# First batch of an mLSTM and Fourier-mixing kernel: recurrent outputs with tokens on partitions, no transposes, three blocks run backwards

## The chip, the core and the metric

The kernel runs on one core of a Trainium2 chip. The metric is the device time of one execution in microseconds (us). One execution on the chip was also recorded by the profiler: its page and its trace are what the text below reads. TensorE is called PE, its weight loads PEld, VectorE DVE, ScalarE ACT, GpSimd POOL, and SyncE, whose queue starts all the DMAs here, SP.

## What is computed

Two blocks follow each other, each over 4 batches of 768 tokens. The first is an mLSTM cell with 8 heads of 40 features. For each token, with a running maximum `m` that keeps the exponentials in range:

```python
m_new  = maximum(f + m, i)
f_stab, i_stab = exp(f + m - m_new), exp(i - m_new)
C = f_stab * C + i_stab * outer(v, k)      # 40 x 40 per head
n = f_stab * n + i_stab * k
y = sigmoid(o_gate) * (C @ q) / maximum(abs(n @ q), 1)
```

The second takes the heads side by side as `x` (768 x 320 for each batch):

```python
u  = x + real(fft(fft(x, axis=seq), axis=features))
un = (u - mean(u)) / sqrt(var(u) + 1e-6)
out = u + maximum(un @ w_ch1, 0) @ w_ch2   # 320 -> 1280 -> 320
```

The weights `w_ch1` and `w_ch2` arrive as 64-bit floats and are turned into 32-bit ones on the chip.

## The kernel before

**The work of one batch.** The recurrence is done in 6 chunks of 128 tokens. For a chunk, `mlstm_scores` multiplies keys by queries (PE), `mlstm_exp` makes the decay weights from gate sums that `spread_max` has put into PSUM by PE (ACT, 8 activations, one for each head), `mlstm_weigh` multiplies the two (DVE), `mlstm_from_state` adds what the state `C` of earlier chunks gives (PE), `mlstm_from_chunk` what the chunk's own tokens give (PE), and `mlstm_to_state` makes the chunk's part of the next state (PE). `mlstm_decay` (POOL) scales the old state. `mlstm_finish` (DVE, five instructions) divides by the normaliser, applies the output gate that `mlstm_tanh` (ACT) has prepared, and writes 128 tokens x 320 features of `x`.

**The first batch is done in another form than the others.** In batches 1 to 3 (`halves_*`) the outputs come out of PE with the tokens on partitions, 41 columns for each head. In batch 0 (`mlstm_*`, planned by `plan_mlstm`, lines 764 to 782) they come out with features on partitions (line 583, weights `C`, 128 query columns moving; line 590, weights `v1`). ACT then copies them to `hT` (`mlstm_heads`, lines 618 to 632) and copies the state (line 614), and PE turns the copy by four transposes (`mlstm_turn`, line 642) before `mlstm_finish` can read it. The old state is added on PE, by a product with the identity (line 605).

**Mixing.** The Fourier transform over the tokens uses the symmetry of cosines and sines: `mix_fold` adds and subtracts chunk pairs (0,5), (1,4), (2,3), whose second members must lie backwards. In `hT` this was done by ACT's copies, and two tokens (0 and 384) were moved there. `mix_seq` and `mix_tail` (tiles `pz`, `pzt`) transform over tokens, `mix_feat` (tile `pu`) over features, `mix_add` (DVE, lines 966 to 980) adds and takes mean and variance, `mix_center` (ACT, line 988) centres, `mix_turn` (PE, tile `put` or `ph`, line 999) turns, and `mix_turn_out` (ACT, line 1004) copies to `uT`. The two layers of the MLP follow (`mlp_in`, lines 1073 and 1082, then `mlp_out`); the chunks 0, 5, 1 make the first half of its columns, 4, 2, 3 the second.

**Order.** The order on each engine is written by hand. `at(slot, phase, fn, ...)` puts a step into a slot, and `run()` issues the steps in order of slot and phase; each engine takes its instructions in that order, and so does SP with the DMAs. PSUM banks for most of batch 0 are handed out by a string of digits, `turn`. The first batch fills slots 0 to 22, its mixing 22 to 31, its MLP starts in slot 31, and the next batch's recurrence starts in slot 32, between the MLP's products. `gates_of_halves` (lines 319 to 392), in steps 0 to 8, prepares gates for batches 1 to 3. It ran in slots 15 to 22. Its step 2 stores to `M_d` and `G_d` in DRAM what the later batches load, as 12 DMAs and one. The weights come in ten pieces, each with a load (SP), `take` (DVE, two instructions), `convert` (ACT, two) and `join` (DVE, three). The tables of the transform, `ds_sb` (1158 KB) and `dd_sb` (642 KB), are loaded by SP in slot 12, and the output gate of chunk 5 in slot 14.

Of the kernel before, what the change touches and what calls it, by code (L numbers as in the profile page):

```python
# [19 lines left out]
L = 128  # L20
# [17 lines left out]
COL = (0, L + 1, 2 * L + 2)  # L38
LAST = 2 * L + 1
# [4 lines left out]
BACKWARDS = (2, 4, 5)  # L44
# [13 lines left out]
def kernel(  # L58
# [30 lines left out]
    ps_s, ps_h = (ps_early.enter_context(tc.tile_pool(name=n, bufs=2, space=PSUM)) for n in ("ps_s", "ps_h"))  # L89

    turn = iter("3210321032120312031230123102112310231023102310231")
# [7 lines left out]
    rest = const.tile([L, 2 * L], FP, name="rest")  # L99
# [16 lines left out]
    C_bufs = [const.tile([L, NP, L], FP, name=f"C{n}") for n in range(3)]  # L116
    states = [t.rearrange("p n t -> p (n t)")[:, i * 2 * L:(i + 1) * 2 * L] for t in C_bufs for i in range(2)]
# [3 lines left out]
    Cd_bufs = [s_last[:, n * NP * D1:(n + 1) * NP * D1].rearrange("p (n m) -> p n m", m=D1) for n in range(2)]  # L121
    hT_bufs = []
# [18 lines left out]
    def idle_products(n, first=False):  # L141
        pw = bank("pi", [L, 2 * L]) if first else ps_s.tile([L, 2 * L], FP, name="pi", tag="ps")
        for i in range(n):
            nc.tensor.matmul(pw, rest[:, 0:L], rest, start=True, stop=True, skip_group_check=True)


    def gates(gp):
# [3 lines left out]
        hT_bufs.extend(gp.tile([L, NP, L + 1], FP, name=f"h{n}") for n in range(2))  # L151
# [6 lines left out]
        M = gp.tile([L, NT, L], FP, name="M")  # L158
# [6 lines left out]
        ident_b, later_b = (gp.tile([L, L], BF, name=n) for n in ("ident_b", "later_b"))  # L165
# [4 lines left out]
        idle_products(3, True)  # L170
        mlstm_load(0, 0)
        make_identity(nc, ident)
        nc.gpsimd.memset(later_b, 0.0)
# [8 lines left out]
        nc.vector.memset(M[:, 0:2], 0.0)  # L182
        for t in C_bufs:
            nc.scalar.copy(out=t.rearrange("p (two n) t -> p two (n t)", two=2),
                           in_=rest.unsqueeze(1).to_broadcast([L, 2, 2 * L]))
# [8 lines left out]
        for t in hT_bufs + Cd_bufs + alone:  # L194
            nc.gpsimd.memset(t, 0.0)
# [21 lines left out]
        def spread_max(b, c, h0):  # L217

            k = chunks[b, c]
            if h0 == 0:  # L220
                k.W = wp.tile([L, H, L], FP, name="W", tag="W")
                k.M = []
            k.M.append(bank("pM", [L, NP, L]))
            nc.tensor.matmul(k.M[-1], ident_b, later_b.unsqueeze(1).to_broadcast([L, NP, L]), start=True, stop=False,
                             skip_group_check=True)
            for h in range(h0, h0 + NP):
                bh = b * H + h
                w, x = (ident[:, bh:bh + 1], M[:, c, :]) if c < 2 else (sel[:, bh:bh + 1], M3[:, c, :])
                nc.tensor.matmul(k.M[-1][:, h - h0, :], w.to_broadcast([w.shape[0], L]), x, start=False, stop=True,  # L229
                                 skip_group_check=True)  # L230

        def parts(s):

            m, rest_ = M[0:BH, s], shift[:, s]
# [5 lines left out]

        def spread_decay(b, c):
            k = chunks[b, c]
            k.G = bank("pG", [L, NP, L])
            for h in range(H):
                r, bh = slice(h % 2 * 64, (h % 2 + 1) * 64), b * H + h
                nc.tensor.matmul(k.G[r, h // 2, :], ident[:, bh:bh + 1].to_broadcast([L, 64]), g[:, c, :],
# [6 lines left out]
        def decay(s):  # L253
            for c in range(s.start, s.stop):
                nc.scalar.activation(out=g[0:BH, c], in_=M[0:BH, c], func=AF.Exp, scale=-1.0, bias=m_in[:, c])

        def columns(s, j):
            pt = ps_h.tile([L, NT, BH], FP, name="pt", tag="ph")
# [6 lines left out]
        maxima(first, M_INIT)  # L265
        pt = columns(first, 0)
# [34 lines left out]
        def decays():  # L301
            dec = gp.tile([BH, BH // 2, NT], FP, name="dec")
            nc.vector.tensor_tensor(out=dec[:, :, 1:],
                                    in0=g[0:BH, 1:, L - 1].unsqueeze(1).to_broadcast([BH, BH // 2, NT - 1]),
                                    in1=spread_sb[:, L:].unsqueeze(2).to_broadcast([BH, BH // 2, NT - 1]), op=OP.mult)
            pd = bank("pd", [L, BH // 2, NT - 1])
            nc.tensor.matmul(pd, spread_sb[:, 0:L], dec[:, :, 1:], start=True, stop=True)
            late["pd"] = pd

        def decays_out():  # L310
            nc.vector.tensor_copy(out=decB[:, 0:NP, 1:NT], in_=late["pd"][:, 0:NP])
# [4 lines left out]
        def gates_of_halves(step):  # L316
# [15 lines left out]
            elif step == 1:  # L332
                m, w = flat_of(M), W.rearrange("p c (i t) -> p c i t", i=2)
                nc.scalar.copy(out=W[:, 0:4:3].rearrange("p c t -> p c t"),
                               in_=bass.AP(tensor=m.tensor, offset=m.offset + 1, ap=[list(m.ap[0]), [HALF, 2], [1, L]]))
                nc.scalar.copy(out=W[:, 1], in_=M[0:BH, 1])
                for c, n in ((2, 2), (4, 1)):
                    src = bass.AP(tensor=m.tensor, offset=m.offset + START[c] + LH - 1,
                                  ap=[list(m.ap[0])] + ([[HALF, 2]] if n > 1 else []) + [[LH, 2], [-1, LH]])
                    nc.scalar.copy(out=w[:, 2:6:3] if n > 1 else w[:, 4], in_=src)  # L340
                nc.gpsimd.tensor_copy(out=W[:, 0:4:3, L - 1:L], in_=late["nexts"][:, 1:5:3])
                nc.gpsimd.tensor_copy(out=W[:, 4, LH:LH + 1], in_=late["nexts"][:, 5])
            elif step == 2:
                nc.scalar.activation(out=late["between"], in_=late["between"], func=AF.Exp)
                for c in range(NT):
                    for i in range(2):
                        t = slice(i * LH, (i + 1) * LH)
                        nc.scalar.activation(out=G[:, c, t], in_=W[:, c, t], func=AF.Exp, scale=-1.0,
                                             bias=late["starts"][:, c, i:i + 1])
# [8 lines left out]
                nc.sync.dma_start(out=G_d[:, H:].rearrange("c p t -> p c t"), in_=G[H:BH])  # L358
# [35 lines left out]
        at(1, FILL + 0.2, parts, last)  # L394
# [9 lines left out]
        for n, (s, phase) in enumerate(((15, FILL + 0.75), (16, FILL + 0.75), (18, FILL + 0.75), (19, FILL + 0.75),  # L404
                                        (18, FILL + 0.8), (19, FILL_PE + 0.5), (20, FILL + 0.75),
                                        (21, FILL_PE + 0.5), (22, FILL + 0.75))):
# [73 lines left out]
    def mlstm_load(b, c):  # L480
# [3 lines left out]
        k.C = [C_bufs[(i + n) % 3] if b == 0 else states[(b * NS + 2 * c + n) % len(states)] for n in range(3)]  # L484
# [6 lines left out]
        k.kn = k.k[:, 0:H * D].rearrange("p (h d) -> p h d", d=D)  # L491
# [9 lines left out]
    def mlstm_load_decay(b, c):  # L501
        k, t = chunks[b, c], slice(0, L)
        if (b, c) != (0, 0):
            k.Gb = gbp.tile([L, NP, L], FP, name="Gb", tag="Gb")
            for hip in range(2):
                h = slice(hip, H, 2) if b == 0 else slice(b * H + hip * NP, b * H + (hip + 1) * NP)
# [45 lines left out]
    def mlstm_decay(b, c):  # L552

        k = chunks[b, c]
        if 0 < c < NT - 1:
            k.Cd = Cd_bufs[c % 2]
            for hip in range(2):
                r, m = slice(hip * 64, hip * 64 + D), slice(hip * 64, hip * 64 + D1)
                d = decB[r, b * NP:(b + 1) * NP, c].unsqueeze(2).to_broadcast([D, NP, D1])
                nc.gpsimd.tensor_tensor(out=k.Cd[r], in0=k.C[0][r, :, m], in1=d, op=OP.mult)  # L560
# [10 lines left out]
    def mlstm_weigh(b, c):  # L571
        k = chunks[b, c]
        for hip in range(2):
            Wv = k.W.rearrange("p (pr two) t -> p pr two t", two=2)[:, :, hip, :]
            nc.vector.tensor_tensor(out=Wv, in0=k.ps[hip], in1=Wv, op=OP.mult)

    def mlstm_from_state(b, c):

        k = chunks[b, c]
        k.ph = ps_h.tile([L, NP, L], FP, name="ph", tag="ph")  # L580
        if c > 0:
            for p in range(NP):
                nc.tensor.matmul(k.ph[:, p, :], k.C[0][:, p, :], k.qg[:, p, :], start=(p == 0), stop=False,
                                 skip_group_check=True)

    def mlstm_from_chunk(b, c):
        k = chunks[b, c]
        for p in range(NP):
            for hip in range(2):
                nc.tensor.matmul(k.ph[hip * 64:hip * 64 + D1, p, :], k.v1[:, 2 * p + hip, :], k.W[:, 2 * p + hip, :],  # L590
                                 start=(c == 0 and p == 0), stop=True, skip_group_check=True)

    def mlstm_to_state(b, c):
        k = chunks[b, c]
        if c < NT - 1:
            add = c > 0
            k.pc = ps_h.tile([L, NP, D1], FP, name="pc", tag="ph")
            for h in range(H):
                r0 = (h % 2) * 64
                nc.tensor.matmul(k.pc[r0:r0 + D, h // 2, :], k.kn[:, h, :], k.vw[:, h, :], start=(h < 2), stop=not add,  # L600
                                 skip_group_check=True)
            if add:
                for hip in range(2):
                    r = slice(hip * 64, hip * 64 + D)
                    nc.tensor.matmul(k.pc[r], ident[:, r], k.Cd, start=False, stop=True, skip_group_check=True)

    def mlstm_gather(b, c):
        k = chunks[b, c]
        if c in SPECIAL:
            nc.scalar.copy(out=hT_bufs[(c - 1) % 2][:, :, L:], in_=k.ph[:, :, 0:1])  # L610
        if c < NT - 1:
            for hip in range(2):
                r, m = slice(hip * 64, hip * 64 + D), slice(hip * 64, hip * 64 + D1)
                nc.scalar.copy(out=k.C[1][r, :, m], in_=k.pc[r])
        mlstm_heads(c, k, k.ph)
        mlstm_tanh(b, c)

    def mlstm_heads(c, k, ph):

        hT, before = hT_bufs[c % 2], hT_bufs[(c - 1) % 2]
        shifted = START[c] % LH
        k.hT = hT[:, :, shifted:shifted + L] if c not in BACKWARDS else hT[:, :, 0:L]
        if c in SPECIAL:
            nc.scalar.copy(out=hT[:, :, 1:L], in_=backwards(ph, L - 1, L - 1) if c in BACKWARDS else ph[:, :, 1:])
# [915 lines left out]
```

## Time and profile before

| | |
|---|---|
| median of 3 runs | 401.58 us (401.5, 401.58, 404.1) |
| the profiled execution, its own time | 402.01 us |
| its span, first to last instruction | 400.3 us |
| mean granted PE clock over the span | 0.991 |
| PE, DVE, ACT, POOL busy | 384.4, 277.3, 178.2, 135.4 us |
| DMA moved | 43.97 MB, mean 110 GB/s |

Times inside the trace are counted from the first instruction. 1.7 us of the profiled execution's own time lie outside the span. In a line of the timeline the first number is the start, the second the length of the group, and what stands in brackets is the idle time of the engine before it and what ended that.

### The profile page before, as it was taken

To read this page: it belongs to the slowest core of one execution; us is meant where nothing else is said; L and a number is where in the kernel's file an instruction comes from. 1 tells how busy PE (TensorE), PEld (TensorE's weight loads), DVE (VectorE), ACT (ScalarE), POOL (GpSimd) and SP (SyncE) were. 2 spreads that over 40 slices of the span, in tenths; PEclk is the share of its full clock that TensorE was granted. 3 is DMA by queue.
4 is the path that set the end of the run, shared out by engine and by line. 5 is a ranking of instruction groups with operands and counts; after the bars stand their busy time and mean duration, and the time that the engine had idled before them with its cause. 6 is when DMAs were issued, how large, how long until landed. Compare 5 with 4: busy or idle time off the path is not lost.

```text
span 400.3 us, 10816 instructions
## 1 busy us (share of the span) xinstructions
PE 384.4 (96%) x4318; PEld 281.2 (70%) x4318; DVE 277.3 (69%) x670; ACT 178.2 (45%) x513; POOL 135.4 (34%) x231
## 2 busy tenths in 40 slices
PE   8999896999889999999999998999999999999996
PEld 6888453556557777755459898856579997556996
DVE  8776963689799546879774688678853785336652
ACT  6978844677533232563542214564440023454000
POOL 6654521676836432263251304562300000020000
PEclk9999996999999999999999999999999999999999
DMA  7987498288776143455000814520000000000000
GB/s 225 295 240 257 104 241 201 73 234 239 239 208 157 61 129 99 155 169 174 7 0 2 215 51 143 182 77 5 0 0 18 18 34 33 2 0 1 34 34 34
DMA packets 22767, 43.97 MB, mean 110 GB/s; under 512 B 3492, under 2 KB 11388, under 8 KB 22588
## 3 DMA queue, kind: packets, MB, share of 16 engines
q1 hardware_dynamic: 22716, 43.27, 36.8%
q8 instruction: 34, 0.56, 0.5%
q14 instruction: 17, 0.14, 0.1%
HBM read 39.16 MB, written 4.10 MB: 108 GB/s over the span
## 4 chain that ended last, share of the span: by engine, by line
PE 73%; DVE 18%; issue 3%; ACT 2%; POOL 2%; DVEq 0%; POOLq 0%; ACTq 0%
PE po L1274 21%; PE pm L1145 14%; PE po L1218 8%; PE pm L1150 5%; PE pu L952 3%; PE ph L549 3%; PE ps L549 3%; PE pm L1082 2%; PE pz L907 2%; DVE so L758 2%; PE put L999 1%; DVE x L761 1%; PE pzt L907 1%; DVE h L1154 1%; PE pM L229 1%
## 5 line engine op out<-in xcount | busy, mean ns | idle before, releaser
L1224 DVE SCALAR_TENSOR_TENSOR x<-po,rstd,x 128x160 f32<-128x160 f32 (+1 forms) x69 | 27.2, 394 | 38.9 <-PE po L1274 36.3
L1154 DVE TENSOR_TENSOR h<-h,pm 128x384 f32<-128x384 f32 x60 | 30.6, 550 | 26.6 <-PE pm L1150 12.1
L545 POOL TENSOR_SCALAR_AFFINE_SELECT W<-W 64x512 f32<-64x512 f32 x36 | 28.1, 780 | 39.3 <-ACT W L520 38.1
L1145 PE MATMUL pm<-uT,w_sb 128*128 128x384 f32 x90 | 37.8, 507 | 0.2 <-DVE uT L1133 0.2
L698 POOL TENSOR_TENSOR C<-C,decB 128x164 f32<-128x164 f32 x33 | 17.9, 542 | 56.2 <-DVE C L705 54.8
L520 ACT ACTIVATE W<-W,colT 128x64 f32<-128x64 f32 x144 | 36.6, 336 | 0.0
L1218 PE MATMUL po<-w_sb,h 128*128 128x320 f32 x120 | 34.1, 435 | 0.0
L1023 POOL TENSOR_TENSOR t<-rstd 128x6 f32<-128x6 f32 x12 | 4.2, 353 | 81.4 <-DVE v L1017 80.9
L530 POOL TENSOR_TENSOR qg<-qk,Gb 128x512 f32<-128x512 f32 x21 | 28.5, 1357 | 7.5 <-DMA Gb<-G_d 7.5
L1082 PE MATMUL pm<-uT,w_sb 128*128 128x384 f32 x80 | 29.9, 509 | 0.0
L1274 PE MATMUL po<-T,S 128*128 128x160 f32 x180 | 28.0, 302 | 1.1 <-DVE x L1224 1.1
L1218 PEld LDWEIGHTS po<-w_sb,h 128*128 128x128 f32 x120 | 22.3, 190 | 9.1 <-issue 0.6
L1274 PEld LDWEIGHTS po<-T,S 128*128 128x128 f32 x180 | 25.4, 190 | 2.7 <-DVE x L1224 1.3
L1150 PE MATMUL pm<-uT,w_sb 64*128 64x384 f32 x120 | 26.3, 511 | 0.4 <-DVE h L1154 0.4
L1274 PE MATMUL po<-w_sb,h 128*128 128x160 f32 x180 | 26.3, 300 | 0.0
L1274 PEld LDWEIGHTS po<-w_sb,h 128*128 128x128 f32 x180 | 25.2, 190 | 1.5 <-DVE x L1224 0.3
L1145 PEld LDWEIGHTS pm<-uT,w_sb 128*128 128x128 f32 x90 | 15.4, 189 | 13.8 <-DVE h L1154 5.9
L1201 ACT ACTIVATE h<-h 128x384 f32<-128x384 f32 x45 | 23.1, 520 | 3.0 <-DVE h L1154 3.0
L988 ACT ACTIVATE uc<-x 128x384 f32<-128x384 f32 x24 | 14.5, 614 | 20.2 <-DVE x L980 20.2
L705 DVE TENSOR_TENSOR C<-C,ps 128x164 f32<-128x164 f32 x33 | 10.5, 317 | 18.0 <-PE ps L549 15.3
L1150 PEld LDWEIGHTS pm<-uT,w_sb 64*128 64x128 f32 x120 | 12.8, 185 | 12.8 <-issue 8.2
L1004 ACT COPY uT<-put 128x384 f32<-128x384 f32 x21 | 9.6, 476 | 26.9 <-PE put L999 26.8
(242 smaller groups left out, 859.5 us busy)
## 6 DMA issues: line engine op xcount, KB each, us to landing
kvt<-in_kv SPq DMA_DIRECT2D x24, 336.0 KB
qk<-in_qkT SPq DMA_DIRECT2D x48, 160.0 KB
raw<-in_w SPq DMA_DIRECT2D x10, 640.0 KB
Gb<-G_d SPq DMA_DIRECT2D x42, 128.0 KB
W<-M_d SPq DMA_DIRECT2D x36, 128.0 KB
so<-in_o SPq DMA_DIRECT2D x24, 160.0 KB
out<-x SPq DMA_DIRECT2D x24, 160.0 KB
ds_sb<-in_dft_s SPq DMA_DIRECT2D x1, 1158.0 KB
```

The lines of the kernel that those rows point to most:

```text
L520: nc.scalar.activation(out=k.W[:, h, :], in_=M, func=AF.Exp, scale=-1.0, bias=colT[:, c, 0, b * H + h:b * H + h + 1])
L530: nc.gpsimd.tensor_tensor(out=k.qg[:, :, t], in0=k.qk[:, 0, :, t], in1=k.Gb[:, :, t], op=OP.mult)
L545: nc.gpsimd.affine_select(out=W, in_=W, compare_op=OP.is_ge, fill=0.0, base=base, pattern=[[0, H], [-1 if back else 1, LH]], channel_multi ...
L549: nc.tensor.matmul(out, w, x, start=start, stop=True, skip_group_check=True)
L1082: nc.tensor.matmul(k.pm[i], w1_block(ch, f // 2 * 2 + i), u[2 * ch], start=(ch == 0 and not ahead), stop=(ch == 1 and ahead), skip_group_c ...
L1145: nc.tensor.matmul(bank, w, u, start=start, stop=True, skip_group_check=True)
L1150: nc.tensor.matmul(bank, w1_rest(i)[rows], mlp_u(gr, 1)[rows], start=False, stop=True, skip_group_check=True)
L1154: nc.vector.tensor_tensor(out=h, in0=h, in1=bank, op=OP.add)
L1201: nc.scalar.activation(out=h, in_=h, func=AF.Relu, scale=-1.0)
L1218: nc.tensor.matmul(k.po[m], hidden(gr, f)[:, i * L:(i + 1) * L], w2_sb[:, f, :], start=(f == 0), stop=(f == NFF - 1))
L1224: nc.vector.scalar_tensor_tensor(out=u, in0=po, scalar=k.rstd[:, c:c + 1], in1=u, op0=OP.mult, op1=OP.add)
L1274: nc.tensor.matmul(po, a[:, f], w[:, f], start=start and f == 0, stop=f == half - 1, skip_group_check=True)
```

## The change

In the first batch the outputs now come out with tokens on partitions, as in the other batches. `mlstm_from_state` and `mlstm_from_chunk` have 128 token columns as weights and 41 columns moving; both halves of the heads lie in one PSUM tile `first_heads_ps`, two banks. The copies to `hT`, the transposes, the product with the identity and the zeroing of the old state buffers are gone. The state is added by DVE (`mlstm_add`), and the old one is scaled by POOL in one instruction where there were two.

The blocks 0, 3 and 4 (before: 2, 4 and 5) now run backwards, and the reversal is made ahead: the queries and the gates' running maxima lie backwards (`queries` on ACT, one DVE copy for block 0, a second mask `later_r`), and the host lays out queries and output gates so. Rows 0 of `x` in blocks 0 and 1, and in 3 and 4, are exchanged by ACT copies of 1 x 320 (`mlstm_rows`). The tables' columns follow the new order, and even and odd rows change places.

The steps of `gates_of_halves` move to slots 6 to 23: the stores to `M_d` from slot 18 to 9, the 12 activations of step 2 become two steps (10 and 11, slots 13 and 16), and the store to `G_d` goes to slot 16. Weight piece 1 is taken and converted in slots 8 and 10 (before 11 and 13) and joined in 18 (before 22), so the load of piece 3 moves from slot 23 to 19, ahead of batch 1's first loads in SP's queue. The folds are done by pairs (2,3), (1,4), (0,5) in slots 17, 17, 18, with two `eo` buffers for one; two of their columns are added straight from `x`. `mix_center` of chunks 4 and 2 moves from their turn's slots to their add's. Weight piece 2 is taken in slots 31 to 33 (before 29, 30, 32).

```diff
-    turn = iter("3210321032120312031230123102112310231023102310231")
+    turn = iter("3210321032"+"13"+"02"+"31"+"301"+"231021"+"1231"+"0231"*4)
-BACKWARDS = (2, 4, 5)
+BACKWARDS = (0, 3, 4)
...
+        def queries():
+            x, y = M[0:BH, 3], Mq[0:BH, 3:5]
+            nc.scalar.copy(out=y[:, :, 1:], in_=bass.AP(tensor=x.tensor, offset=x.offset + L - 1,
+                                                        ap=[list(x.ap[0]), [L, 2], [-1, L - 1]]))
+            nc.scalar.copy(out=y[:, :, 0:1], in_=M[0:BH, 3:5, 0:1])
+            nc.scalar.copy(out=Mq[0:BH, 5], in_=M[0:BH, 5])
...
-        at(1, FILL + 0.2, parts, last)
+        at(1, FILL + 0.2, parts, slice(2, 3))
+        at(2, FILL + 0.6, queries)
+        at(4, FILL + 0.2, parts, slice(3, NT))
...
-        for n, (s, phase) in enumerate(((15, FILL + 0.75), (16, FILL + 0.75), (18, FILL + 0.75), (19, FILL + 0.75),
-                                        (18, FILL + 0.8), (19, FILL_PE + 0.5), (20, FILL + 0.75),
-                                        (21, FILL_PE + 0.5), (22, FILL + 0.75))):
+        for n, s, phase in ((0, 6, FILL + 0.75), (1, 8, FILL + 0.75), (2, 9, FILL + 0.75), (4, 10, FILL + 0.8),
+                            (10, 13, FILL + 0.3), (11, 16, FILL + 0.1), (5, 16, FILL_PE + 0.5), (3, 17, FILL + 0.5),
+                            (6, 18, FILL + 0.2), (7, 22, FILL_PE + 4.5), (8, 23, FILL + 0.2)):
...
     def mlstm_from_state(b, c):
-        k.ph = ps_h.tile([L, NP, L], FP, name="ph", tag="ph")
-        if c > 0:
-            for p in range(NP):
-                nc.tensor.matmul(k.ph[:, p, :], k.C[0][:, p, :], k.qg[:, p, :], start=(p == 0), stop=False,
-                                 skip_group_check=True)
+        n = NP * D1
+        k.ph = first_heads_ps[:, :, c % 2 * n:(c % 2 + 1) * n].rearrange("p hip (m d) -> p hip m d", d=D1)
+        k.pc = halves_state(first_heads_ps[:, c % 2, 2 * n:])
+        for p in range(NP) if c > 0 else ():
+            for hip in range(2):
+                r = slice(hip * 64, hip * 64 + D)
+                product(k.ph[:, hip, p, :], k.qg[r, p, :], k.C[0][r, p * D1:(p + 1) * D1], p == 0)
     def mlstm_from_chunk(b, c):
-                nc.tensor.matmul(k.ph[hip * 64:hip * 64 + D1, p, :], k.v1[:, 2 * p + hip, :], k.W[:, 2 * p + hip, :],
-                                 start=(c == 0 and p == 0), stop=True, skip_group_check=True)
+                h = hip * NP + p
+                product(k.ph[:, hip, p, :], k.W[:, h, :], k.v1[:, h, :], c == 0 and p == 0)
     def mlstm_to_state(b, c):
+                product(k.pc[hip * 64:hip * 64 + LH, p, :], k.k[:, h * D:h * D + LH], k.vw[:, h, :], False)
+    def mlstm_add(b, c):
+        if c == 0:
+            nc.vector.tensor_copy(out=halves_state(k.C[1]), in_=k.pc)
+        else:
+            nc.vector.tensor_tensor(out=halves_state(k.C[1]), in0=halves_state(k.C[1]), in1=k.pc, op=OP.add)
+    def mlstm_rows(b, c):
+        spare, x = s_last[0:1, 0:DM], xs[b][0:1, :, 0:DM]
+        if c in SPECIAL:
+            nc.scalar.copy(out=x[:, c - 1], in_=x[:, c])
+            nc.scalar.copy(out=x[:, c], in_=spare)
+        else:
+            nc.scalar.copy(out=spare, in_=x[:, c])
...
     def plan_mlstm
-            at(s + 1 if end else s + 2, FILL - 0.4 if end else FILL, mlstm_weigh, b, c)
+            at(s + 1, FILL + (0.2 if end else -0.4), mlstm_weigh, b, c)
-            at(s + 3, FILL_PE + 3, mlstm_to_state, b, c)
-            at(s + 3 if end else s + 4, FILL, mlstm_gather, b, c)
-            t, x = ((8, 9), (11, 12), (13, 14), (16, 16.5), (17, 18), (18, 20))[c]
-            at(t, FILL_PE + (2.5 if c < 4 else 1), mlstm_turn, b, c, c < 4)
-            at(x, FILL + 0.05, mlstm_finish, b, c)
+            if not end:
+                at(s + 3, FILL_PE + 3, mlstm_to_state, b, c)
+                at(s + 4, FILL - 0.3, mlstm_add, b, c)
+            at(*((16, FILL + 0.02) if end else (s + 4, FILL - 0.25)), mlstm_tanh, b, c)
+            t, phase = ((5, 0.6), (7, 0.05), (10, 0.05), (13, 0.05), (16, -0.2), (18, 0))[c]
+            at(t, FILL + phase, mlstm_finish, b, c)
+        for c, t, phase in ((0, 6, 0.3), (1, 8, 0.3), (3, 14, 0.3), (4, 16, 0.15)):
+            at(t, FILL + phase, mlstm_rows, b, c)
...
-        ends(nc.vector, fe[:, p], 0, every)
+        nc.vector.tensor_tensor(out=fe[:, p, 0:NC:HALF_D], in0=x[:, c, 0:NC:HALF_D], in1=x[:, m, 0:NC:HALF_D], op=OP.add)
...
             if b == 0:
-                at((s0 - 4, s0 - 2, s0)[j], FILL_PE + 4, mix_seq, b, p, (0, 1))
-                at((s0 - 2, s0 - 2, s0)[j], FILL_PE + 4, mix_tail, b, p)
+                at((17, 17, 18)[j], FILL + (0.1, 0.3, 0.3)[j], mix_fold, b, p)
+                s, phase = ((17, 3), (18, 3), (22, 4))[j]
...
-            at(t, FILL + 0.1, mix_center, b, c)
+            at(*((a, FILL + 0.25) if b == 0 and c in (4, 2) else (t, FILL + 0.1)), mix_center, b, c)
...
-    eo_p = pool("eo", 1)
+    eo_p = pool("eo", 2)
...
-    when = [((2, 0.7), (4, 0.5), (6, 0.6)), ((11, 0.7), (13, 0.7), (22, 0.6)), ((29, 0.7), (30, 0.7), (32, 0.6))]
+    when = [((2, 0.7), (4, 0.5), (6, 0.6)), ((8, 0.7), (10, 0.6), (18, 0.6)), ((31, 0.7), (32, 0.7), (33, 0.6))]
```

## The prediction, made before the changed kernel ran

> **What bounds the kernel now.** I read the busy shares in slices first, then busy time and clock by stage, then the timelines of PE, ACT and DVE in the first 76 us, because everything that the change touches ends there.
>
> ```profile
> PE   8999896999889999999999998999999999999996
> ...
> PEclk9999996999999999999999999999999999999999
> ```
>
> ```profile
> 42.00:58.00 16.00, 15.48 (x75) 8.36 (x73) 12.40 (x32) 11.65 (x41) 5.97 (x9) 1.00 0.73 189
> 58.00:76.00 18.00, 14.44 (x104) 7.84 (x103) 8.80 (x18) 10.09 (x29) 5.62 (x9) 0.81 0.68 169
> ```
>
> ```profile
> 63.10:69.90 6.80, 5.96 (x75) 3.73 (x76) 1.30 (x3) 2.73 (x9) 1.78 (x3) 0.50 0.82 184
> ```
>
> The columns of a stage are its ends and length, then busy us of PE, PEld, DVE, ACT and POOL, the granted clock, and the DMA's share and rate. PE is 96% busy over the span; one slice of the 40 has a dip, and there the clock fell to 0.50 for 6.8 us. The timelines show why (DVE, ACT, PE):
>
> ```profile
> 60.48 0.46 DVE L435 TENSOR_SCALAR e<-raw 128x640 uint32<-128x640 uint32 x1
> ```
>
> ```profile
> 60.97 0.83 ACT L442 ACTIVATE e<-e,ebias 128x640 uint32<-128x640 uint32 x1 [2.83 <-DVE e L435]
> ...
> 63.29 0.60 ACT L988 ACTIVATE uc<-x 128x384 f32<-128x384 f32 x1
> ```
>
> ```profile
> 58.20 2.20 PE L1082 MATMUL pm<-uT,w_sb 128*128 128x384 f32 x6
> 63.94 0.90 PE L999 MATMUL ph<-ident,uc 128*128 128x128 f32 x3 [3.54 <-ACT uc L988]
> 64.63 1.49 PE L1082 MATMUL pm<-uT,w_sb 128*128 128x384 f32 x2
> ```
>
> ACT stood in its queue behind the conversion of weight piece 2, which waited for DVE's sixth add; the centring of the fourth chunk, free since 58.15, came only at 63.29. PE idled 3.54 us, and what it did until 70 ran at half clock: the two records of line 1082 from 64.63 stand for 1.49 us, while two others take 0.81 at 72.47.
>
> In the recurrence PE works without gaps, 5.0 us for each chunk:
>
> ```profile
> 23.37 1.06 PE L583 MATMUL ph<-qg,C 128*128 128x128 f32 x8
> 24.36 1.16 PE L569 MATMUL ps<-qk 40*128 40x128 f32 x16
> 25.45 1.07 PE L590 MATMUL ph<-W,kvt 128*41 128x128 f32 x16
> 26.36 0.47 PE L600 MATMUL pc<-vw,kvt 128*40 128x41 f32 x16
> 26.66 0.45 PE L605 MATMUL pc<-s_last,ident 128*40 128x164 f32 x4
> ...
> 27.94 0.60 PE L642 MATMUL px<-ident,h 128*128 128x128 f32 x4
> 28.39 1.06 PE L583 MATMUL ph<-qg,C 128*128 128x128 f32 x8
> ```
>
> From start to start: state 0.99, scores 1.09, own tokens 0.91, new state 0.30, identity 0.39, gate sums 0.89, transposes 0.45.
>
> **Part 1, PE's work for a chunk.** Identity (0.39) and transposes (0.45) go. The products with 128 columns as weights and 41 moving have no row of their own. Their 16 passes cost at least the streaming of 41 columns (the later batches' form, 32 in 0.60 us over four tiles at once, gives about 0.3 us for 16), at most 16 loads of 0.19 us one after the other, 3.0 us. The nearest row with a load of 128 columns and little streaming is this:
>
> ```profile
> 43.38 0.56 PE L380 MATMUL p<-ident,a 32*128 32x32 f32 x6
> 43.78 0.57 PE L382 MATMUL p<-w_sb,spread_sb 32*128 32x192 f32 x2
> ```
>
> Six in 0.40 us are 0.067 each; line 260 gives 0.084. I take 0.075: 1.2 us for the own tokens (+0.3), 0.8 for the state, whose two row halves alternate (-0.2), 0.5 for the new state with 64 columns for 40 (+0.2). A chunk comes to 4.5 us of PE for 5.0.
>
> The Trainium skill ("TensorE: Matmul & The Clock Gate", section LDWEIGHTS) puts a load at its columns divided by 1.2, in ns: 107 for 128 columns, and so an estimate of 1.7 us for 16. The row says 0.067 to 0.084, so I don't use it; by it a chunk would take PE 5.8 us, and the sum would end near 398.7.
>
> **Part 2, the chain that takes over.** With less to do, PE waits in the recurrence for ACT and DVE, whose queues have got the gate work. I carry the queues forward in their new order, with durations of the timelines (an exp group of 8: 2.1, `mlstm_finish` 1.7, weigh 1.3, join 2.4, tanh 0.4, a conversion 1.4).
>
> Start: one more DVE copy of block 0's maxima ahead of the long scan, a 32x128 operation (0.28 beside it): +0.25. DVE now weighs chunk 1, copies the state and scales queries before it makes `dec`: from 13.6, 1.6 (take), 1.3, 0.25, 0.6, 0.45, so 17.6 where it was 15.8. PE's `pd`, and the gate sums of chunk 2 behind it, wait 1.7 us.
>
> DVE from 17.6: 0.7 to `decB` and its wait on PE, 1.7, 0.6, join 2.4, 0.1, weigh 1.3, state 0.3, finish of block 1 1.7: 26.4. On ACT the exchange of block 1's row stands behind that and ahead of chunk 3's exps: two copies of 0.4 (as the 128x320 tanh), four copies of step 1 1.2 (28.4), exps 2.2 (30.6), tanh and conversion of piece 1 1.8 (32.4), exps of chunk 4 2.1 (34.5). DVE: second weigh 0.6, state 0.3, finish 1.7 (37.1). ACT: row 0.4, exps of chunk 5 2.1, tanh 0.4 (40.0). DVE: the end of finish 4 1.0, weigh 1.3 (42.3). PE: own tokens 1.2, 43.5. Before, that product ended at 40.7. The removed ACT copies (C 0.61 and h 0.58 for each chunk) are paid back by this; PE idles about 2.4 us ahead of chunk 3's state.
>
> **Part 3, the folds.** Nothing is turned after 43.5, where 41.5 to 42.0 and one more finish came before. But in SP's queue the 12 stores to `M_d` (4.17 us of issue) now stand ahead of the tables and of chunk 5's output gate, and wait for ACT's copies of step 1 (28.4, with POOL's 28.7): issue of the stores to 32.9, `Gb` to 34.1, tables and gate at 34.9 to 35.7. Before they were issued at 28.36 to 30.32, and the DMAs ran at 248 to 388 GB/s until 38. 1.96 MB at 250 to 300 GB/s take 6.7 to 8.0 us: the gate lands at 42.4 to 43.7; I take 43.2. ACT's tanh of chunk 5 waits for it, with six activations of the gates (1.5) and the row exchange of block 4 (0.8) behind: 45.9. DVE's pair (1,4) waits for that exchange, and the finish of chunk 5 stands behind the pair: 0.9, 1.7, and 1.6 for pair (0,5): 50.1. Before, the last fold ended at 47.8 and `pz` started at 48.60. So +1.5. The two-column copies, 0.74 and 0.60 us while POOL worked and 0.17 alone, become adds; I take 0.1 each, and that lies in the sum.
>
> From `pz` to the MLP's first product PE had 9.6 us of work without a gap; the same instructions with waits of 0.2 for three centrings: 10.0. The MLP starts at 60.1 (58.20 before): +1.9.
>
> **Part 4, the stall goes.** The centrings of chunks 4 and 2 now stand right behind their adds, ahead of batch 1's exps and the conversion, and piece 2 is taken after the adds. From the MLP's start to the end of its first product of the second half (76.19 before, 18.0 us): 2.0, turn 0.4, 1.6, batch 1's scores and state 1.0, turn 0.4, 2.0, a wait of 0.5 for the sixth centring (late next, behind the conversion), turn 0.4, 1.6, 2.0: 11.9 us at full clock. -6.1.
>
> Behind that the order is that of before. Both PE (38.6 of 41 us) and DVE (36.6) are nearly full from 76 to 117, so a lead stays, neither growing nor shrinking; what covers it are DVE's 8.5 us of idle between 63 and 76.
>
> **Sum** against the profiled execution (402.01, 0.4 above the median, span 400.3 and 1.7 around it): +1.9 - 6.1 = -4.2. On the median: 401.6 - 4.2 = **397.4**, its own range 395.4 to 399.4.
>
> **Rivals.**
>
> *The gate of chunk 5 is there in time* (DMA quicker, or the copies of step 1 earlier). Then ACT isn't held, `pz` starts when the finish allows, about 48.2, and the sum loses 1.9; if DVE's chain runs half a us quicker too: 395. For it: the rate was 388 GB/s at 34 to 36. Against: four engines' steps ahead of that issue.
>
> *A new gap halves the clock.* PE idles about 2.4 us ahead of chunk 3's state and as much ahead of pair (1,4). In the profile the clock fell 2.7 us after PE stopped at 60.4, and the 6 us of work that followed at 0.50 cost 3. One such drop: 400.4. The Trainium skill (same page, Part 1) says that an idle window of about 3.4 us, free-running, throttles to half; the trace's 2.7 us is shorter, so no gap under 3.4 is safe by the row, while by the rule these two would stay warm.
>
> *Loads don't overlap* (the slower end). If each load of 128 columns holds PE for the 0.19 us that its record shows, own tokens take 3.0, state 1.5, new state 1.6, a chunk 8.1 us; carried forward, that ends 9.5 us behind before: 411. It decides from about 0.135 us for a load, where gain and loss cancel. Against it: the records of 0.190 at line 1274 stand 0.136 apart, those of 0.136 at line 380 0.067 apart.
>
> *Batch 1's loads come late.* The load of piece 3 stands ahead of them and waits for the join of piece 1, now about 52.6; they started at 45.2 before. At 240 GB/s chunk 0 has landed by 59.5 for exps due at 61, and chunk 2 by 71 for 74. Three us later, and most of the gain is lost: 401.
>
> **How the numbers follow.** About 1% (4 us) is what a measurement of this kernel can tell from no change. Forecast 0.45, of which 0.30 beyond 1%; gate in time 0.25, faster; clock 0.12 and late loads 0.06, within 1%; serial loads 0.12, slower. Faster 0.55, same 0.32, slower 0.13. The range leaves out the serial loads and the far ends: 392.5 to 402.
>
> **What would show it.** Right: no wait of PE on the centring near 62, clock 1.00 from 60 to 76, exps of chunk 3 waiting on the row exchange, the product of chunk 5 near 43.5, tanh of chunk 5 waiting on a DMA. Wrong: passes of the new products over 0.1 us apart; a chunk period of 4.5 held by PE; a clock of 0.50 before 60; DVE or POOL waiting on `Gb`, `W` or `raw` between 60 and 80.

## The result, and the profile after

The changed kernel takes 428.74 us (median of four runs, 423.13 to 429.21) against 401.62 for the kernel before: ratio 1.0628, 95% interval 1.0546 to 1.0710. The forecast was 397.4, faster, with a range of 392.5 to 402: wrong in sign and size. The profiled execution is the quickest of the four, 423.13 us with a span of 421.4 (+21.1 on that of before). One run each of e4, e9, e10 and e11 was disturbed and is left out of the times below; the trace of e4 is of that run.

The two lines of the profile's page, busy tenths and granted clock in 40 slices, answer to those of before:

```profile
PE   8889899999998999999999999899999999999996
...
PEclk9985556999999999999999999999999999999999
```

The dip of one slice is gone from where it was, and five slices in the recurrence and up to the transforms have taken its place. The stages (ends, length, busy us of PE, PEld, DVE, ACT and POOL, then the clock, DMA share and GB/s):

```profile
18.00:42.00 24.00, 19.99 (x195) 17.31 (x197) 14.15 (x33) 12.65 (x44) 10.03 (x22) 0.76 0.55 164
42.00:58.00 16.00, 14.59 (x108) 13.19 (x106) 4.04 (x8) 4.75 (x18) 1.68 (x2) 0.50 0.27 104
58.00:76.00 18.00, 18.00 (x88) 12.08 (x87) 11.09 (x27) 5.79 (x22) 3.88 (x7) 0.63 0.16 50
```

Before, the clock was 1.00 from 18 to 58 us. Now it is at half from 20.1 to 23.5 and from 33.7 to 71.3. From 42 to 58 PE is the only engine with much to do: it is busy 14.59 of 16 us, at half speed. PE's timeline in the recurrence:

```profile
15.31 1.98 PE L564 MATMUL hb<-kvt,W 128*128 128x41 f32 x16
17.22 0.67 PE L564 MATMUL hb<-vw,kvt 128*64 128x41 f32 x16
19.65 0.43 PE L320 MATMUL pd<-dec,spread_sb 32*128 32x64 f32 x2 [1.76 <-DVE dec L316]
...
31.12 1.09 PE L564 MATMUL hb<-C,qg 40*128 40x41 f32 x16 [1.48 <-DVE x L741]
32.04 1.14 PE L581 MATMUL ps<-qk 40*128 40x128 f32 x16
33.11 3.12 PE L564 MATMUL hb<-kvt,W 128*128 128x41 f32 x16
...
39.94 1.93 PE L564 MATMUL hb<-C,qg 40*128 40x41 f32 x16 [0.88 <-DVE x L741]
...
51.52 1.93 PE L564 MATMUL hb<-C,qg 40*128 40x41 f32 x16 [1.41 <-DVE x L741]
...
63.41 3.63 PE L564 MATMUL hb<-kvt,W 128*128 128x41 f32 x16
```

The first two lines give the price of the new products at full clock, from start to start: the own tokens' 16 passes take 1.91 us, 0.119 each; the line from 63.41 is the same product at half clock. The brackets are PE's waits; before, the one for `pd` was 0.43 us, and no state product waited over 0.23. The state products wait for the finish of the chunk before, and ACT's queue for the same instruction (DVE, then ACT):

```profile
30.58 0.49 DVE L741 TENSOR_TENSOR x<-hb,so 128x320 f32<-128x320 f32 x1
```

```profile
31.16 0.46 ACT L748 COPY x<-x 1x320 f32<-1x320 f32 x1 [6.83 <-DVE x L741]
...
51.41 0.46 ACT L751 COPY s_last<-x 1x320 f32<-1x320 f32 x1 [9.28 <-DVE x L741]
```

The MLP starts at 84.62 (58.20 before, +26.4). From there on the change does what was forecast: no product waits for a centring, and the first product of the second half ends near 96.1, 11.5 us on, where it took 18.0:

```profile
84.62 2.20 PE L1080 MATMUL pm<-uT,w_sb 128*128 128x384 f32 x6
86.66 0.49 PE L990 MATMUL ph<-ident,uc 128*128 128x128 f32 x3
86.99 0.81 PE L1080 MATMUL pm<-uT,w_sb 128*128 128x384 f32 x2
```

**Where the 21.1 us come from.** Half clock lasted 40.96 us up to the MLP and 6.83 before; the 34.1 us more do 17.1 us of full-clock work, so up to 17.1 us went there. A chunk costs PE 1.91 + 0.91 + 1.09 + 0.60 + 0.89 = 5.4 us at full clock, for 5.0: 1.9 in five chunks. PE's waits in the recurrence are 5.5 us (1.76, 1.48, 0.88 and 1.41), for 1.4 before. The stall of 3.54 is gone. 17.1 + 1.9 + 4.1 - 3.5 = 19.6; the last 1.5 us stay open. In the other three runs the mean clock was 0.932 over a span of about 427, which is 58 us at half for 41 here; 17 us more at half are worth up to 8.5 us, and these runs took 5.5 to 6 us longer.

### The profile page after: what moved, and what is told of

Read it like the earlier page. It is cut to its first block, busy times and chain, and to the rows that moved or that the text cites. A ratio compares the mean times of both kernels' runs of the same rounds, so it can differ in the third digit from the quotient of the medians.

```text
span 421.4 us, 10814 instructions
## 1 busy us (share of the span) xinstructions
PE 404.2 (96%) x4318; PEld 299.4 (71%) x4318; DVE 282.3 (67%) x678; ACT 172.8 (41%) x501; POOL 132.8 (32%) x229
## 3 DMA queue, kind: packets, MB, share of 16 engines
q1 hardware_dynamic: 21564, 43.27, 34.1%
## 4 chain that ended last, share of the span: by engine, by line
PE 62%; DVE 10%; issue 2%; POOL 1%; ACT 1%; DVEq 0%; POOLq 0%
PE po L1272 19%; PE pm L1143 15%; PE po L1216 8%; PE pm L1148 5%; PE ph L564 3%; PE pu L943 3%; PE ps L564 2%; PE pm L1080 2%; PE pz L898 2%; DVE so L738 1%; PE put L990 1%; PE pzt L898 1%; DVE h L1152 1%; DVE C L685 1%; PE pm L1071 1%
## 5 line engine op out<-in xcount | busy, mean ns | idle before, releaser
L1152 DVE TENSOR_TENSOR h<-h,pm 128x384 f32<-128x384 f32 x60 | 30.6, 550 | 26.8 <-PE pm L1148 12.4
L1216 PE MATMUL po<-w_sb,h 128*128 128x320 f32 x120 | 34.1, 435 | 0.0
L545 POOL TENSOR_TENSOR qg<-qk,Gb 128x512 f32<-128x512 f32 x21 | 27.5, 1311 | 17.1 <-DMA kvt<-in_kv 17.1
L1143 PEld LDWEIGHTS pm<-uT,w_sb 128*128 128x128 f32 x90 | 15.4, 189 | 13.9 <-DVE h L1152 5.9
L551 POOL TENSOR_TENSOR vw<-kvt,colT 128x328 f32<-128x328 f32 x23 | 19.9, 863 | 5.5 <-DVE colT L287 2.8
L1080 PEld LDWEIGHTS pm<-uT,w_sb 128*128 128x128 f32 x80 | 14.0, 189 | 10.4 <-issue 3.0
```

Source lines behind the costliest of these rows:

```text
L545: nc.gpsimd.tensor_tensor(out=k.qg[:, :, t], in0=k.qk[:, 0, :, t], in1=k.Gb[:, :, t], op=OP.mult)
L1080: nc.tensor.matmul(k.pm[i], w1_block(ch, f // 2 * 2 + i), u[2 * ch], start=(ch == 0 and not ahead), stop=(ch == 1 and ahead), skip_group_c ...
L1143: nc.tensor.matmul(bank, w, u, start=start, stop=True, skip_group_check=True)
L1152: nc.vector.tensor_tensor(out=h, in0=h, in1=bank, op=OP.add)
L1216: nc.tensor.matmul(k.po[m], hidden(gr, f)[:, i * L:(i + 1) * L], w2_sb[:, f, :], start=(f == 0), stop=(f == NFF - 1))
```

## The experiments

The question is why the clock fell and stayed down. Theory A: the new products stream too little. Theory B: PE waits too often. Theory C came out of the first eight experiments.

**e1: the kernel before, with Part 4 alone.**

```diff
-            at(t, FILL + 0.1, mix_center, b, c)
+            at(*((a, FILL + 0.25) if b == 0 and c in (4, 2) else (t, FILL + 0.1)), mix_center, b, c)
-    when = [..., ((29, 0.7), (30, 0.7), (32, 0.6))]
+    when = [..., ((31, 0.7), (32, 0.7), (33, 0.6))]
```

> The kernel before, with one part of the change alone: the centrings of chunks 4 and 2 behind their adds, and weight piece 2 taken in slots 31 to 33. Both theories (A: the clock falls because the new products stream too little; B: it falls because PE waits more often) expect what the prediction's part 4 said: no wait of PE on a centring near 62, clock 1.00 from 60 to 76, 401.6 - 6.1 = 395.5. If the lead is lost again between 76 and 117, 400 or more.

396.80 us against 402.91, ratio 0.9861 (0.9841 to 0.9882); clock 1.00 over the whole profiled run. So the stall and the half clock behind it were worth about 5.6 us, as Part 4 said, and this kernel beats both.

```profile
58.00:76.00 18.00, 17.18 (x243) 9.87 (x243) 14.79 (x27) 13.32 (x39) 10.58 (x13) 1.00 0.66 186
```

**e2: the kernel after, own-token products of chunks 1 to 5 turned round** (41 columns as weights, 128 streamed; the sums land transposed, so the output is not the reference's).

```diff
+                if c > 0:
+                    out = first_heads_ps[hip * 64:hip * 64 + D1, hip, c % 2 * NP * D1:c % 2 * NP * D1 + L]
+                    product(out, k.v1[:, h, :], k.W[:, h, :], False)
+                    continue
```

> The changed kernel, with the own-token products of chunks 1 to 5 turned round: 41 columns as weights and 128 moving, as before, into the same PSUM tile (the sums are then not the reference's). All waits of PE on the finish of the chunk before stay. Theory A (too little streaming): the clock stays 1.00 from 34 to 71, at most one window of 0.50 behind the wait for the decay, and the MLP starts near 60: 398 to 402. Theory B (the waits): the clock is at 0.50 for most of 34 to 71 as in the changed kernel, 418 or more.

415.95 us, ratio 1.0331 (1.0300 to 1.0363): between the forecasts of the two theories, so it decides nothing. The clock still halves, first at 18.3 us, but comes back three times before the transforms.

**e3: the kernel before, own-token products of chunks 1 to 5 in the new form** (again not the reference's sums).

```diff
+                if c > 0:
+                    product(k.ph[:, p, hip * 64:hip * 64 + D1], k.W[:, 2 * p + hip, :], k.v1[:, 2 * p + hip, :], False)
+                    continue
```

> The kernel before, with the own-token products of chunks 1 to 5 in the new form alone: 128 columns as weights, 41 moving (the sums are then not the reference's). No wait is added. 16 passes cost 1.9 us for 0.9 at full clock, so +5 us. Theory A (too little streaming): the clock falls to 0.50 within the recurrence, 410 or more. Theory B (the waits): the clock stays at 1.00 there, 406 to 407.

408.29 us, ratio 1.0141 (1.0064 to 1.0219); its two runs, 405.71 and 410.87, lie 5 us apart, so the time decides nothing. The trace is of the longer one. Its own-token passes also cost 0.119 us (27.19 to 29.10), so the price belongs to the product and not to its surroundings. The clock stays at 1.00 until 47.5 us, the end of the recurrence, and is then at half for 6.8. I took that as a point for theory B, too early, as e6 shows.

```profile
27.19 1.98 PE L549 MATMUL ph<-kvt,W 128*128 128x41 f32 x16
29.10 0.51 PE L603 MATMUL pc<-vw,kvt 128*40 128x41 f32 x16
```

**e4: the kernel after, with two dense products (512 f32 columns) ahead of each chunk's scores.**

```diff
+        for t in k.ps if c > 0 else ():
+            product(t, ident, ident.unsqueeze(1).to_broadcast([L, NP, L]), True)
```

> The changed kernel, with two more products of 512 moving columns ahead of each chunk's scores from chunk 1 on, overwritten by the scores: about 2 x 0.85 us of streaming more for each chunk, 8.5 us in all if nothing hides it. Theory A (too little streaming): the clock stays at or near 1.00, and the time falls from 423 to 429 to 402 to 410. Theory B (the waits): the waits stay, so does the clock at 0.50, and the time is 430 or more.

430.08 us, one run, so without a ratio. The first half-clock stretch moved from 20.1 us to 33.2. The waits stayed (the first is 1.23 us for 1.76), and the clock fell at the second, of 1.48 us.

**e5: the kernel after, with PE's waits filled** (three more spreads into each tile of the maxima for chunks 3 to 5, eight short products ahead of `pd`).

```diff
+            for _ in range(3 if c > 2 else 0):
+                product(k.M[-1], ident_b, later.unsqueeze(1).to_broadcast([L, NP, L]), True)
...
+            for _ in range(8):
+                product(pd.rearrange("p n c -> p (n c)"), ident, ident[:, 0:BH // 2 * (NT - 2)], True)
```

> The kernel after, with TensorE's waits filled by products that change nothing: three more 512-column bf16 products ahead of each spread of the maxima for chunks 3 to 5, and eight 64-column products ahead of the decays' product. Theory B (the clock falls because TensorE waits 0.9 to 1.8 us at four places): the granted clock stays 1.00 through the recurrence, the MLP starts near 64 us, and the time is 402 to 408 us. If the waits are not the cause, the clock still halves near 20 and 34 us and the time stays at 420 us or more.

412.66 us, ratio 1.0263 (1.0218 to 1.0309): 16 us better than the kernel after, for more work. The time lies between the two forecasts. The waits are down to 0.5 us at most, yet the clock halves at 40.8 and again at 51.0.

**e6: the kernel after, waits taken away by order alone; e7: half of that.**

```diff
-        at(4, FILL + 0.5, decays)
+        at(4, FILL - 0.35, decays)
...
-            at(s + 2 if end else s + 3, FILL_PE, mlstm_from_state, b, c)
+            at(s + 2 if end else s + 3, FILL_PE + (1 if end else 2.5), mlstm_from_state, b, c)
```

(e7 has the second edit only.)

> The kernel after, with two changes of order that take the waits away and add no work: each chunk's state products stand behind the next chunk's scores, so that the scores cover the finish of the chunk before, and the decays' tables are made one step earlier on VectorE. Theory B (the waits halve the clock): clock 1.00 up to the MLP, no wait of TensorE over 0.6 us before 45 us, MLP start 61 to 64 us, time 398 to 404 us. Theory A (the new products stream too little, with or without waits): the clock halves near 34 us as before, MLP start over 75 us, time 416 us or more.

> The kernel after with only one of the two changes of order: state products behind the next chunk's scores. The 1.76-us wait for the decays near 18 us stays. Theory B: a half-clock stretch of 3.4 us at about 20 us stays (it costs some 1.7 to 3 us) and the long one from 34 us goes: time 401 to 408 us. If one early wait is enough to lose the clock up to the MLP, 415 us or more. Theory A: 416 us or more.

e6: 416.68 us, ratio 1.0363 (1.0330 to 1.0397). e7: 425.69, ratio 1.0587 (1.0534 to 1.0640). Theory B falls with e6. Up to 45 us only one wait is left, of 0.39 us, and the clock halves at 28.2 and stays down for 37.5 us; PE is busy 23.61 of the 24 us around the fall. In e7, which keeps the wait of 1.76 us, it falls at 18.0 and, after one stretch at full clock, again at 28.2. From e6, the wait of 0.39, the product behind it, in which the clock falls, and the stage:

```profile
26.77 1.09 PE L564 MATMUL hb<-C,qg 40*128 40x41 f32 x16 [0.39 <-DVE x L741]
27.79 3.32 PE L564 MATMUL hb<-kvt,W 128*128 128x41 f32 x16
```

```profile
18.00:42.00 24.00, 23.61 (x233) 21.49 (x231) 13.46 (x31) 12.59 (x43) 9.27 (x21) 0.71 0.75 234
```

**e8: the kernel before, with two waits put in** (VectorE copies the weights of chunks 2 and 3 onto themselves three times).

```diff
+        for _ in range(3 if b == 0 and c < 2 else 0):
+            W = chunks[b, c + 2].W
+            nc.vector.tensor_copy(out=W, in_=W)
```

> The kernel before with two waits put in: behind the finish of chunks 0 and 1 VectorE copies the weights of chunk 2, then 3, onto themselves three times, so that TensorE waits about 1.5 to 2 us ahead of their own-token products near 25 and 31 us. Nothing else is changed. If waits alone halve the clock (theory B in its strict form): a half-clock stretch of at least 3.4 us begins within 4 us of the first wait, and the time rises by more than the waits, to 407 us or more. If the clock falls only where waits and the new sparse products come together: clock 1.00 in the recurrence and the time up by at most the two waits, 402 to 406 us.

407.67 us, ratio 1.0139 (1.0105 to 1.0173). The waits came out at 2.83 and 1.80 us; the first one brings a half-clock stretch of 3.41 us from 30.0, the second none. The time and the first wait are what theory B forecast; the second wait, which brings nothing, is not.

```profile
28.86 1.07 PE L590 MATMUL ph<-W,kvt 128*41 128x128 f32 x16 [2.83 <-DVE W L764]
...
37.33 1.07 PE L590 MATMUL ph<-W,kvt 128*41 128x128 f32 x16 [1.80 <-DVE W L764]
```

**Theory C, from the records.** In all these traces every stretch of granted clock between two changes is a multiple of 3.413 us. I cut each trace on that grid, into 36 cells from the first change on, and for each cell added up PE's records, each spread evenly over its time: rows/128 x weight columns/128 x columns streamed, a bf16 column counted as 0.417 ns and an f32 one as 0.833 (512 bf16 columns stand 0.22 us apart, 386 f32 ones 0.37; the rest is counted as overhead). The sum over 3.413 us is the share of the array in use. A cell under about 0.35 is followed by one at half clock, others by full clock. The bound was chosen on the ten traces up to e8, where 8 of 360 cells go wrong (9 to 11 when the grid is moved by 0.2 us either way). Sorted by PE's busy time instead, with the best bound, 59 go wrong, and by the columns streamed alone, without rows and weight columns, 26. Some cells from the start of the recurrence on, each share with the clock of the cell that follows:

```
kernel   from us: share -> next clock
before   29.0: .58 -> 1.0   32.4: .70 -> 1.0   56.3: .81 -> 1.0   59.7: .18 -> 0.5
after    16.6: .14 -> 0.5   20.1: .37 -> 1.0   26.9: .40 -> 1.0   30.3: .25 -> 0.5   44.0: .16 -> 0.5   67.8: .46 -> 1.0
e6       17.9: .52 -> 1.0   21.3: .38 -> 1.0   24.8: .33 -> 0.5   28.2: .18 -> 0.5   62.3: .42 -> 1.0
e8       23.2: .61 -> 1.0   26.6: .19 -> 0.5   30.0: .42 -> 1.0   33.5: .40 -> 1.0
```

The same sum for one chunk at full clock gives 3.45 us in 5.0 before, 0.69 of the array, and 2.27 us in 5.4 after, 0.42. Most of the fall is the state product (0.85 us of full-array work before, 0.17 after) and what was removed, transposes (0.43) and identity (0.17); the own tokens are worth 0.55 in both forms, but take 1.91 us for 0.91. So the new recurrence runs just above the bound, and a cell with a wait in it, or one that holds state and own-token products only (0.19 and 0.29), can fall under it. At half clock the same chunk takes twice as long and uses 0.21 on the average. Single cells differ: the one from 20.1, full of gate sums, used 0.37, and full clock came back; of the ten from 33.7 on none used more than 0.29, until the dense transforms at 66.8. This is why the first wait put into the dense kernel (e8) costs one cell, and a wait here eleven, 37.5 us.

**e9 and e10: one added work, two shapes.** Both add bf16 products of 512 columns that change no result, as in e5, but also into the score tiles and around chunk 5: about 8.6 us of them, and short ones ahead of `pd`. In e9 they use 128 rows by 128 columns (n = 128), in e10 32 by 32 (n = 32).

```diff
+        def extra(out, times):
+            for _ in range(times):
+                product(out[0:n], ident_b[0:n, 0:n], later_b[0:n].unsqueeze(1).to_broadcast([n, NP, L]), True)
```

> The kernel after, with products added that change no result and use the whole array (128 rows by 128 columns, 512 columns streamed, bf16, about 0.21 us each at full clock): two ahead of each spread of the maxima and two into each score tile from chunk 2 on, four ahead of chunk 5's state products and four ahead of its own-token products, and eight short ones in the wait for the decays. Some 8 us of products in all. Theory C (the clock is set for each stretch of 3.41 us by the share of the array that the stretch before it used, rows times columns times columns streamed, and halves under about 0.35): clock 1.00 up to the MLP, MLP start 65 to 71 us, time 403 to 410 us, in spite of the added work. Theory B (waits of TensorE): waits of 0.5 to 1.5 us remain ahead of state products and the clock halves, 416 us or more.

> The same added products at the same places with the same 512 columns streamed, on 32 rows by 32 columns of the array, one sixteenth of it: TensorE is kept busy just as long. Theory C: the share of the array stays under 0.35, the clock halves from about 20 or 34 us up to the transforms, MLP start over 82 us, time 422 us or more, at least 12 us above the dense twin. A theory in which TensorE only has to be busy or streaming: clock 1.00 as in the dense twin, and a time within 3 us of it.

e9: 423.84 us, ratio 1.0536 (1.0497 to 1.0575). e10: 441.91, ratio 1.0954 (1.0889 to 1.1019), 18 us more for the same streaming. The stage from 18 to 42 us, e9 first:

```profile
18.00:42.00 24.00, 22.55 (x234) 17.11 (x234) 14.24 (x33) 12.65 (x44) 10.03 (x22) 1.00 0.59 165
```

```profile
18.00:42.00 24.00, 24.00 (x160) 16.07 (x158) 10.23 (x25) 7.70 (x28) 7.35 (x20) 0.57 0.45 137
```

PE is busier in e10, 24.00 of 24 us, and has a clock of 0.57 for 1.00; from 14 to 92 us it never waits, at a mean clock of 0.54. That PE is busy, or streams, is not what counts. One drop in e10, from 17.2 to 27.5, begins before the first added product: its cell used 0.33, the like of it in e9 0.36. The long one, from 30.9 to 92.3, is the thin products' own. The e9 forecast of 403 to 410 us failed all the same: its clock holds through every cell down to 0.36, and then the cell from 47.4 uses 0.13, around this wait and these products, and the clock is lost from 50.8 to 71.3:

```profile
48.83 1.09 PE L575 MATMUL hb<-C,qg 40*128 40x41 f32 x16 [1.37 <-DVE x L758]
49.85 2.77 PE L575 MATMUL hb<-kvt,W 128*128 128x41 f32 x16
```

**e11: e9 with that one cell mended.**

```diff
-            extra(k.M[-1], 2 if c > 1 else 0)
+            extra(k.M[-1], 4 if c == NT - 1 else 2 if c > 1 else 0)
...
-        if c == NT - 1:
+        if c >= NT - 2:
             late_fill[0](ps_s.tile([L, NP, L], FP, name="psx", tag="ps"), 4)
```

> The dense kernel with the one stretch mended that used 0.14 of the array (47.5 to 50.9 us: a wait of 1.37 us, then state and own-token products of chunk 4): two more whole-array products ahead of each spread of chunk 5 and four ahead of chunk 4's own-token products, some 1.7 us of work more. Theory C: no stretch before the MLP under 0.35, clock 1.00 throughout the recurrence, MLP start 67 to 72 us, time 405 to 412 us: 12 us or more under the kernel that does less. Theory B (waits), or a limit on how long the recurrence can run at all: the clock still halves between 30 and 55 us, 420 us or more.

414.89 us, ratio 1.0320 (1.0275 to 1.0366): 9.0 us less than e9 with 1.7 us more work, and 13.9 less than the kernel after with 48 products of 0.216 us added, 10.4 us in all. The smallest share from 15 us to the MLP is 0.40, and the clock is 1.00 throughout, with waits of 0.62, 0.84 and 0.52 us left:

```profile
18.00:42.00 24.00, 22.54 (x238) 17.11 (x238) 13.68 (x32) 12.60 (x43) 9.55 (x21) 1.00 0.61 176
42.00:58.00 16.00, 15.48 (x163) 11.45 (x161) 9.08 (x21) 7.78 (x29) 4.20 (x6) 1.00 0.26 100
58.00:76.00 18.00, 17.12 (x85) 10.12 (x84) 11.33 (x31) 6.93 (x21) 1.38 (x4) 1.00 0.52 143
```

The clock came out as theory C has it; my time for it, 405 to 412, was 3 us too low, and the MLP's start 4 too early (75.8 for 67 to 72). Over the three traces e9 to e11, made after the bound was chosen, the rule goes wrong in 2 of 108 cells, and the rule by busy time in 28. Over all thirteen traces: all 69 cells under 0.25 were followed by half clock, 30 of 45 between 0.25 and 0.37, and 2 of 354 above (both 0.37).

## Why the prediction was wrong, step by step

- **Part 1, the passes: mis-sized.** The prediction took 0.075 us for a pass with 128 columns of weights and 41 streamed, from records whose weights have 128 columns too, but only 32 rows; it measured 0.119 at full clock, in after and in e3. Own tokens 1.91 us for 1.2, state 0.91 for 0.8, new state 0.60 for 0.5: a chunk 5.4 us for 4.5, where before it was 5.0. The change saves PE nothing. The figure that was set aside was the better one: the Trainium skill ("TensorE: Matmul & The Clock Gate", section LDWEIGHTS) gives 107 ns for a load of 128 columns, and the trace has 119 a pass. The prediction puts a chunk at 5.8 us by that figure without showing how; scaled from 75 to 107 ns, its three terms of 2.5 us come to 3.6 and the chunk to about 5.5, as an estimate, for 5.4 measured.
- **The clock: the step that failed.** "A new gap halves the clock" had 0.12, and was priced as one drop that costs 3 us. The drop was priced by what came behind it in the kernel before, dense work that brings the clock back after 6.8 us. Here the work itself was under the bound at half speed, and the second of two drops held for 37.5 us: in all 40.96 us at half, up to 17.1 us lost. The working asked how long PE would wait and how long each product would last, never how much of the array the new products use: 0.42 for 0.69. (The chances of same and slower, given as 0.32 and 0.13, add up to 0.33 and 0.12.)
- **The rule for the clock**, weighed in that rival: the Trainium skill (same page, Part 1) speaks of a free-running window of about 3.4 us, idle or busy. The window agrees: all stretches are multiples of 3.413 us. "Idle" does not: of 338 cells in which PE was busy 97% of the time or more, 70 were followed by half clock.
- **Part 2, the chain: the wait for `pd` right by luck** (1.76 us, 1.7 forecast), **the rest late.** `dec` was ready at 19.6, not 17.6 (the terms given add up to 17.8), and PE, with its own tokens mis-sized, came to `pd` late as well. The finish of block 1 ended at 31.07, not 26.4, and chunk 3's exps at 35.2, not 30.6. Half clock from 20.1 to 23.5 is part of that, and DVE's part of a finish that scales the gate, 0.49 us alone, took 0.96 to 1.49 beside POOL. A wait was missed altogether: a state product waits for the finish of the chunk before, which reads the other half of the same PSUM tile. e6 shows that the scores can cover it (0.39 us left of 1.48 at chunk 2; the 1.41 at chunk 4 stays). Whether tiles in separate banks would free it wasn't tried.
- **Part 3, the folds: not tested by the runs.** `pz` starts at 66.84 for 50.1, but it comes behind a chain that was late for the reasons above; the tanh of chunk 5 does not wait for its DMA. The two-column adds, taken at 0.1 us, took 0.47 and 0.48 while POOL worked and 0.16 alone.
- **Part 4: right.** 11.5 us for 11.9 from the MLP's start; alone, in e1, it gives 0.9861.
- **What it would be at full clock** is only worked out: e11 less its 10.4 us of added products is 404.5 us, and more if some of them only fill waits. So without the clock the change would, by this, still have ended slightly slower than before, and nearly 8 us behind e1: Parts 1 to 3 give away more than Part 4 brings.
- What stays open: the rows alone, without the columns of the weights, fit the cells as well (10 of 468 wrong by either), so which of the two counts isn't settled. Nor is whether the values of the data matter, why some cells between 0.29 and 0.37 fall the other way, and why the runs of one kernel differ in clock (after: 0.951 once, 0.932 three times); each kernel has one trace.

## What to carry to other kernels

Before turning a product round to save transposes, work out what share of the array the stage will use per 3.4 us at full clock, and again at half. Here no cell above 0.38 lost the clock, and under 0.37 it was at risk; count the poorest stretch and not the mean, for a mean of 0.42 had cells of 0.14 and 0.25. A stage that is under the bound at half speed stays slow until denser work comes. Price a product that streams few columns by the size of its weights and not by its streaming: a pass of 41 columns took 0.119 us with 128 x 128 weights, and 0.038 with 128 x 64. Where an experiment shows the clock down, filler of the full array's shape tells whether the clock is the cause; filler of a thin shape streams as long and brings nothing.

## What the runs showed of the hardware that was not expected

- The granted clock follows the share of PE's array in use in the 3.413-us cell before (69 of 69 cells under 0.25 went to half, 2 of 354 above 0.37 did), or the rows alone, and not the time that PE is busy: e10 ran at 0.57 from 18 to 42 us while busy all the time.
- The shape of added work counts, at equal streaming: e9 and e10 differ by 18 us (423.84 and 441.91) in nothing but the rows and columns of the added products.
- Adding 10.4 us of useless dense products made the kernel after 13.9 us faster (428.74 to 414.89).
